# Attention steps 9 to 14 of a fused attention and MLP kernel: three batches of two in place of five visits, and four transpositions in other places

## The chip, the core and the metric

The kernel runs on one core of a Trainium2 chip. The metric is the device time of one execution in microseconds (us). The engines, with the short names of the profile: PE (TensorE, matrix products; PEld is its weight loads), DVE (VectorE), ACT (ScalarE), POOL (GpSimd) and SP (SyncE, which here only issues DMAs). PE writes to PSUM, of which the kernel uses eight banks; DVE and ACT take the results out of it to SBUF.

## What is computed

Linear attention with a decay per head, and an MLP on its output. For 4 batches, 8 heads, 768 positions and head size 64, in blocks of 64 positions:

```python
intra = np.einsum('bhic,bhjc->bhij', qb, kb) * Dmask[None]
intra = np.einsum('bhij,bhjd->bhid', intra, vb)
inter = np.einsum('bhid,bhde->bhie', qb * lam_pow[None], kv_state)
out[:, :, sl] = intra + inter
kv_state = lam_block * kv_state + np.einsum('bhsd,bhse->bhde', kb * rev_pow, vb)
...
h = x @ w_in                      # x: (3072, 512), w_in: (512, 2048)
g = 0.5 * h * (1.0 + np.tanh(c * (h + 0.044715 * h * h * h)))
return g @ w_out                  # w_out: (2048, 512)
```

`x` is the attention output, one row for each batch and position, one column for each head and channel.

## The kernel before, in words

**Steps.** Attention goes in 24 steps (0 to 23). Step s stands for a superblock of 256 positions (s // 2; three to a batch) and one half of the heads (s % 2). A step needs, in this order:

- `load_step(s)`: DMAs of q, k and v on SP's queue, into four buffers each.
- `cast_q(s)` on DVE (line 281, q times a decay, to fp16), `cast_k(s)` on ACT (line 293), `scale_v(s)` on POOL (line 265, v times the inverse decay). `prep_qk(s)` is both casts.
- `stage_t(s)`: eight transpositions on PE (line 309) of q and k into one PSUM bank, then two copies to the tile qkT: q's half on ACT (line 316), k's half on DVE (line 317).
- `scores(s)`: 16 small matmuls (64x64 weights, line 341) into two banks; `causal(s)`: two products with the mask on DVE (line 351), into PT.
- the outputs of a step s: products of v and PT (line 391, or 451 in a burst) and of the state u and q (404 or 413, 479 or 489). Steps in the set NARROW do the second with eight 64x64 matmuls (four for the first superblock of a batch), behind a wait of PE; the others with up to four 128x128 ones. The outputs of s are made one visit later than the scores of s.
- K products of step n (line 376, or 466), which `update(n, c)` adds to the running state on DVE (lines 538, 541), from which POOL makes u (lines 549, 556). `update(n, 0)` is done at the end of a visit, `U(n)` is `update(n, 1)`.
- `x_out`: ACT copies the outputs to xT (lines 518, 520), from which the MLP reads.

**Visits.** `R(n, s)` does the scores, the mask and the K products of step n, and the outputs of step s, in four banks. `burst(ns, ss)` does the same for two steps n and one or two steps s: four banks of scores, two of outputs (O), two of K products, then the masks of both, `x_out` and `update(n, 0)`.

**The MLP as filler.** The MLP is cut into pieces of about 0.87 us on PE, which stand in a list, `filler`; `fill(n)` emits the next n. `queue_group(g)` appends the pieces of a group once its last step is through (group 2 is steps 6 and 7, group 3 is steps 8 to 11, group 4 is steps 12 to 15). A group of one superblock has eight pieces of the first MLP product (line 604), each followed by a GELU on ACT (line 608), and seven pieces of the second (line 683). The second product is done in seven products in place of eight, from sums: `sum_g` (DVE, line 653) makes sums of GELU results and is tied to certain pieces (`behind`): for group 2 to the sixth to eleventh. The pieces of the second product, by their number m, are 1, 2, 5, 6, 3, 7, 4; the bank X0 of 1 serves 6, 7 and 4 too, and is held until 4 is done. DVE adds to the outputs at lines 725 and 731. `sum_win` (DVE, line 150) makes sums of the input weights, needed by later groups, in whose pieces (lines 787 to 817) the first product too is done from sums (line 766 makes those of x), with GELUs at line 805 and additions on DVE at 809.

**Order.** Every instruction is pinned: on each engine, the program's order is the order in the queue. The order of everything is written out by hand in the body of the function (lines 984 to 1203): stage_t, fill, casts, visits, updates, one after another. An engine that waits holds what stands behind it.

Of the kernel before, what the change touches and what calls it, by code (L numbers as in the profile page):

```python
# [15 lines left out]
def kernel(  # L16
# [259 lines left out]
    def cast_q(s):  # L276
        q32 = ld32[s][0]
        tqk = a16p.tile([P, 2, 2, HH, D], FP16, tag="qk16", name=f"qk16_{s}")
        tq, tk = tqk[:, 0], tqk[:, 1]
        q_eng = nc.gpsimd if s == 3 else nc.vector  # L280
        pin(q_eng.tensor_tensor(wide(tq), q32[:], decay(dq, s), ALU.mult))  # L281
        if s == 0:
            inverse(halves[0])
            odd(halves[1])
            inverse(halves[1])
        a16[s] = (tq, tk)

    def cast_k(s):
        tk, k32 = a16[s][1], ld32[s][1]
        if s == 4:  # L290
            pin(nc.vector.tensor_copy(out=wide(tk), in_=k32[:]))
        else:
            pin(nc.scalar.activation(out=wide(tk), in_=k32[:], func=AF.Copy))  # L293
# [5 lines left out]
    def stage_t(s):  # L299
        tq, tk = a16[s][:2]  # L300
        if s < 4:
            Tps = [ps_M.tile([P, 2, 2, P], FP16, tag="M", name=f"Tps{i}") for i in range(2)]
        else:
            Tps = ps_M.tile([P, 2, 2, 2, P], FP16, tag="M", name="Tps")
        for i, t in enumerate((tq, tk)):
            to = Tps[i] if s < 4 else Tps[:, i]
            for hp in range(2):
                for j in range(2):
                    pin(nc.tensor.transpose(to[:, j, hp, :], t[:, j, 2 * hp : 2 * hp + 2, :],  # L309
                                            ident[:]))  # L310
        o = qkp.tile([P, 2, 2, 2, P], FP16, tag="qkT", name=f"qkT_{s}")
        if s < 4:
            pin(nc.scalar.activation(out=o[:, 0], in_=Tps[0][:], func=AF.Copy))
            pin(nc.vector.tensor_copy(out=o[:, 1], in_=Tps[1][:]))
        elif s > 7:
            pin(nc.scalar.activation(out=o[:, 0], in_=Tps[:, 0], func=AF.Copy))  # L316
            pin(nc.vector.tensor_copy(out=o[:, 1], in_=Tps[:, 1]))  # L317
        elif s in (5, 6):
            pin(nc.scalar.activation(out=o[:], in_=Tps[:], func=AF.Copy))
        else:  # L320
            pin(nc.vector.tensor_copy(out=o[:], in_=Tps[:]))
        qkT[s] = o
# [105 lines left out]
    def burst(ns, ss, *mix, ahead=None):  # L428


        narrow = bool(NARROW & set(ss))
        for i, n in enumerate(ns):
            scores(n)
            if ahead and i == 0:
                ahead()
        O = [ps_M.tile([P, 2, 2, P], FP32, tag="M", name=f"O{c}") for c in range(2)]
        seen = set()

        def start(kind, c, hl):
            new = (kind, c, hl) not in seen  # L440
            seen.add((kind, c, hl))
            return new

        qTs = [qkT.pop(s) for s in ss]
        for i, s in enumerate(ss):
            PT, tv = PTs.pop(s), a16.pop(s)[2]
            for hp in range(2):
                for jk in range(2):
                    for c, hl in TILES:
                        to = hl ^ narrow * c  # L450
                        mm = nc.tensor.matmul(  # L451
                            O[c][half64(to), i, hp, :], tv[half64(c), jk, 2 * hp + hl, :],
                            PT[half64(c), hl, hp, jk, :], start=start("O", c, to), stop=False,
                            skip_group_check=True)
                        pin(mm)
        if ns:
            K = [ps_M.tile([P, 2, P], FP32, tag="M", name=f"K{c}") for c in range(2)]
        for i, n in enumerate(ns):
            _, tk, tv = a16[n]
            last = (n // 2) % NSB == NSB - 1  # L460
            for jk in range(2):
                for hp in range(2):
                    for c, hl in TILES:
                        if c == 1 and last:
                            continue
                        pin(nc.tensor.matmul(
                            K[c][half64(hl), i, hp * D : hp * D + D],
                            tk[half64(c), jk, 2 * hp + hl, :], tv[half64(c), jk, 2 * hp + hl, :],
                            start=start("K", c, hl), stop=(jk == 1), skip_group_check=True))
            Kps[n] = [t[:, i] for t in K]  # L470
        if narrow:
            behind(mm)
        for i, s in enumerate(ss) if narrow else ():
            u = [us.pop(key, None) for key in ((s - 2, 1), (s, 0))]
            for hp in range(2):
                for c, hl in TILES:
                    if u[c] is None:
                        continue
                    pin(nc.tensor.matmul(
                        O[c][half64(hl ^ c), i, hp, :], u[c][half64(hl), hp, :],  # L480
                        qTs[i][half64(hl), 0, :, hp, half64(c)], start=False, stop=True,
                        skip_group_check=True))
        for i, s in enumerate(ss) if not narrow else ():
            for c in range(2):
                if c == 0 and (s // 2) % NSB == 0:
                    continue
                u = us.pop((s, 0) if c else (s - 2, 1))
                for hp in range(2):
                    pin(nc.tensor.matmul(O[c][:, i, hp, :], u[:, hp].rearrange("p l d -> p (l d)"),
                                         qTs[i][:, 0, :, hp, half64(c)], start=False, stop=True,  # L490
                                         skip_group_check=True))
        for n in ns:
            causal(n)
        for batch in ((ss,) if narrow or not ns else [(s,) for s in ss]):
            i = ss.index(batch[0])
            x_out(batch, [t[:, i : i + len(batch)].rearrange("p i h t -> p (i h t)") for t in O],
                  swapped=narrow)
        sbg = ss[-1] // 2
        g, i = group_of[sbg]
        if ss[-1] % 2 == 1 and i == len(groups[g]) - 1:  # L500
            queue_group(g, *mix)
        for n in ns:
            update(n, 0)

# [449 lines left out]
    def fill(n):  # L954
        for _ in range(min(n, len(filler))):
            filler.pop(0)()
# [23 lines left out]
    def U(n):  # L980
        update(n, 1)
# [94 lines left out]
    scale_v(9)  # L1076
    fill(2)

    FILL = {8: (2, 0, 0, 0), 9: (1, 2, 1, 2), 10: (0, 1, 1, 3), 11: (0, 1, 1, 3), 12: (0, 2, 1, 3)}
    stage_t(8)  # L1080
    for n, (a, b, c, d) in FILL.items():
        fill(a + (n == 10))
        if n == 8:
            cast_q(n + 2)
            fill(1)
            cast_k(n + 2)
        else:
            prep_qk(n + 2)
        if n < 11:
            load_step(n + 4, "qkv" if n < 10 else "qk")  # L1090
        if n == 11:
            scale_v(13)
            load_step(14, "v")
            load_step(16, "qk")
        elif n == 9:
            scale_v(11)
        elif n == 10:
            scale_v(12)
            load_step(15, "qk")
        elif n == 12:  # L1100
            scale_v(14)
        fill(b + (n == 8) - (n == 10))
        R(n, n - 1, keep=n == 8)
        fill(c)
        if n == 8:
            update(n, 0)
            scale_v(n + 2)
            fill(2)
        U(n)
        if n == 12:  # L1110
            prep_qk(15)
            load_step(15, "v")
            load_step(16, "v")
            scale_v(15)
        stage_t(n + 1)
        fill(d)
        if n > 8:
            sum_win((n - 7) // 2, (n - 1) % 2, nc.vector)

    cast_qk(16)  # L1120
    load_step(17, "qk")
    load_step(17, "v")
    store_pair(1)
    for send in kept_stores[0]:
        send()
    scale_v(16)
    fill(1)
    stage_t(14)
    fill(2)
    burst((13, 14), (12,))  # L1130
    fill(1)
    U(13)
    U(14)
    load_ahead(18)
    fill(1)
    stage_t(15)
    fill(2)
    stage_t(16)
    fill(2)
    burst((15, 16), (13, 14), ahead=lambda: (prep_qk(17), scale_v(17)))  # L1140
    for send in kept_stores[1]:
        send()
# [29 lines left out]

    burst((18, 19), (16, 17))
    prep_v(21)
    fill(2)
    U(18)
    U(19)
    fill(2)
    stage_t(20)
    fill(2)  # L1180
    stage_t(21)
    prep_qk(22)
    fill(2)
    burst((20, 21), (18, 19), 11, 4)
    fill(3)
    U(20)
    U(21)
    fill(20)
    prep_qk(23)
    fill(23)  # L1190
    prep_v(22)
    prep_v(23)
    fill(3)
    stage_t(22)
    fill(4)
    stage_t(23)
    fill(6)
    burst((22, 23), (20, 21))
# [33 lines left out]
```

## Time and profile before

| what | value |
|---|---|
| median of 3 runs | 206.25 us (206.2 to 206.27) |
| the profiled execution | 205.97 us |
| its span, first to last instruction | 204.2 us |
| ACT, busy share of the span | 65% |
| POOL, busy share of the span | 32% |
| HBM, mean over the span | 164 GB/s |

The page of the profile lists busy times, the chain of work that ended last (followed back from the last instruction), and groups of instructions by line. The timeline lists instructions in order of time: start in us from the span's start, time taken by the (merged) entry, engine, line, tiles, shapes and count, and in brackets the idle time ahead of it with what ended it. Matmuls are pipelined, so an entry of PE is longer than the distance to the next start; durations of PE work are therefore taken from start to start, and mostly those of DVE too. The windows view gives, for a stretch, its length and then the busy time of PE, PEld, DVE, ACT and POOL with the number of instructions in brackets, the granted PE clock, and the DMA share and rate.

The attention visits in PE's timeline begin at 58.75 (R(8,7)), 64.48 (R(9,8)), 69.38 (R(10,9)), 75.15 (R(11,10)), 81.80 (R(12,11)), 89.77 (burst (13,14)/(12)), 97.19 (burst (15,16)/(13,14)), 107.16 (R(17,15)), 121.19 (burst (18,19)/(16,17)), 130.62 (burst (20,21)/(18,19)) and 161.12 (burst (22,23)/(20,21)). The transpositions of steps 9 to 16 begin at 61.32, 66.22, 71.12, 76.89, 83.61, 87.51, 92.75 and 94.92; those of 20 to 23 at 126.18, 128.35, 155.15 and 157.34.

### The profile page before, as it was taken

To read this page: it belongs to the slowest core of one execution; us is meant where nothing else is said; L and a number is where in the kernel's file an instruction comes from. 1 tells how busy PE (TensorE), PEld (TensorE's weight loads), DVE (VectorE), ACT (ScalarE), POOL (GpSimd) and SP (SyncE) were. 2 spreads that over 40 slices of the span, in tenths; PEclk is the share of its full clock that TensorE was granted. 3 is DMA by queue.
4 is the path that set the end of the run, shared out by engine and by line. 5 is a ranking of instruction groups with operands and counts; after the bars stand their busy time and mean duration, and the time that the engine had idled before them with its cause. 6 is when DMAs were issued, how large, how long until landed. Compare 5 with 4: busy or idle time off the path is not lost.

```text
span 204.2 us, 6246 instructions
## 1 busy us (share of the span) xinstructions
PE 197.8 (97%) x2597; PEld 146.2 (72%) x2597; DVE 151.4 (74%) x307; ACT 133.7 (65%) x264; POOL 66.3 (32%) x85
## 2 busy tenths in 40 slices
PE   8979999999999999999999999999999999999993
PEld 2556544467888888655588865668889788888882
DVE  5897525789799979969989545999566898467720
ACT  2673867297866896787856389763868665679221
POOL 6684132457407423715224505037001130002000
PEclk9999999999999999999999999999999999999999
DMA  6999999999999477598504480000011200020205
GB/s 180 290 333 389 382 389 370 292 290 290 295 305 249 137 206 216 169 321 226 152 7 121 149 249 6 0 3 0 0 42 64 102 9 0 3 103 2 106 3 203
DMA packets 45916, 33.95 MB, mean 166 GB/s; under 512 B 1728, under 2 KB 38848, under 8 KB 45888
## 3 DMA queue, kind: packets, MB, share of 16 engines
q1 hardware_dynamic: 45344, 33.30, 54.8%
q8 instruction: 20, 0.33, 0.7%
q10 hardware_dynamic: 544, 0.26, 0.4%
q14 instruction: 8, 0.07, 0.1%
HBM read 27.26 MB, written 6.29 MB: 164 GB/s over the span
## 4 chain that ended last, share of the span: by engine, by line
PE 85%; SPq 4%; DMA 4%; ACT 3%; DVE 2%; issue 1%
PE Hps L604 20%; PE MX L683 17%; PE MY L683 9%; PE HX L787 7%; PE O2ps L619 7%; PE MW L683 4%; PE Tps L309 4%; DMA wi<-in_moe_w_in_dram 4%; SPq L69 4%; PE HY L787 4%; PE S L341 3%; PE Hps L886 3%; PE HW L787 2%; DVE gs L653 1%; PE O L451 1%; PE OK L391 1%
## 5 line engine op out<-in xcount | busy, mean ns | idle before, releaser
L604 PE MATMUL Hps<-xT,w_in 128*128 128x512 f16 (+1 forms) x288 | 52.0, 332 | 0.0
L604 PEld LDWEIGHTS <-w_in 128*128 128x128 f16 x288 | 27.3, 98 | 17.6
L608 ACT ACTIVATE gT<-Hps 128x512 f16<-128x512 f32 x56 | 32.7, 598 | 8.9 <-PE Hps L604 8.5
L683 PEld LDWEIGHTS <-gs 128*128 128x128 f16 x320 | 31.1, 98 | 3.7
L351 DVE TENSOR_TENSOR PT<-S,mask 128x512 f16<-128x512 f32 x48 | 30.4, 683 | 3.4 <-PE S L341 3.1
L265 POOL TENSOR_TENSOR v<-v,dv 128x512 f16<-128x512 f32 x24 | 28.2, 1179 | 7.8 <-DMA v<-in_v_dram 4.7
L683 PEld LDWEIGHTS <-gT 128*128 128x128 f16 x240 | 23.1, 98 | 3.5 <-ACT gT L608 0.2
L556 POOL TENSOR_TENSOR u<-t,lumask 128x256 f16<-128x256 f32 x21 | 14.9, 723 | 26.7 <-DVE t L541 15.6
L683 PE MATMUL MX<-w_sum,gs 128*128 128x256 f16 x160 | 21.4, 273 | 0.0
L549 POOL TENSOR_TENSOR u<-t,lamu 128x128 f16<-128x128 f32 x19 | 9.0, 477 | 33.4 <-DVE t L541 27.0
L293 ACT ACTIVATE qk<-k 128x512 f16<-128x512 f32 x23 | 14.4, 626 | 7.7 <-DMA k<-in_k_dram 7.4
L281 DVE TENSOR_TENSOR qk<-q,dq 128x512 f16<-128x512 f32 x23 | 18.4, 798 | 0.7 <-DMA q<-in_q_dram 0.7
L740 POOL TENSOR_TENSOR o<-u,q 128x512 f32<-128x512 f32 (+1 forms) x5 | 5.6, 1119 | 40.0 <-issue 35.1
L653 DVE TENSOR_TENSOR gs<-gT 128x1024 f16<-128x1024 f16 (+1 forms) x24 | 17.1, 721 | 0.5 <-ACT gT L608 0.5
L317 DVE COPY qkT<-Tps 128x512 f16<-128x512 f16 x16 | 6.8, 423 | 12.3 <-ACT qkT L316 12.3
L309 PEld LDWEIGHTS <-qk 128*128 128x128 f16 x192 | 12.8, 99 | 4.2 <-DVE qk L281 0.7
L309 PE MATMUL Tps<-ident,qk 128*128 128x128 f16 x192 | 15.2, 222 | 0.5 <-POOL qk L281 0.5
L619 PE MATMUL O2ps<-w_out,gT 128*128 128x512 f16 x64 | 14.6, 379 | 0.0
L787 PEld LDWEIGHTS <-ws 128*128 128x128 f16 x128 | 12.4, 98 | 1.7 <-DVE xs L766 0.3
L520 ACT ACTIVATE xT<-OK 128x256 f16<-128x256 f32 x22 | 8.7, 454 | 5.1 <-PE OK L413 2.7
L705 ACT ACTIVATE u<-MX 128x256 f32<-128x256 f32 x18 | 6.9, 384 | 7.1 <-PE MX L683 7.1
L619 PEld LDWEIGHTS <-gT 128*128 128x128 f16 x64 | 6.1, 98 | 6.6
(107 smaller groups left out, 350.6 us busy)
## 6 DMA issues: line engine op xcount, KB each, us to landing
q<-in_q_dram SPq DMA_DIRECT2D x24, 256.0 KB, 5.0
k<-in_k_dram SPq DMA_DIRECT2D x24, 256.0 KB, 5.1
v<-in_v_dram SPq DMA_DIRECT2D x23, 256.0 KB, 5.3
out_dram<-o SPq DMA_DIRECT2D x23, 256.0 KB, 2.7
wo<-in_moe_w_out_dram SPq DMA_DIRECT2D x4, 1024.0 KB, 9.5
wi<-in_moe_w_in_dram SPq DMA_DIRECT2D x4, 512.0 KB, 7.8
wi<-in_moe_w_in_dram SPq DMA_DIRECT2D x2, 1024.0 KB, 12.5
v<-in_v_dram ACTq DMA_DIRECT2D x1, 256.0 KB, 4.2
```

The lines of the kernel that those rows point to most:

```text
L265: pin(nc.gpsimd.tensor_tensor(wide(tv[:]), ld32[s][2][:], decay(dv, s), ALU.mult))
L281: pin(q_eng.tensor_tensor(wide(tq), q32[:], decay(dq, s), ALU.mult))
L293: pin(nc.scalar.activation(out=wide(tk), in_=k32[:], func=AF.Copy))
L309: pin(nc.tensor.transpose(to[:, j, hp, :], t[:, j, 2 * hp : 2 * hp + 2, :], ident[:]))
L351: pin(nc.vector.tensor_tensor(t[:, hl].rearrange("p b c d -> p b (c d)"), Sps[:].rearrange("p b c d -> p b (c d)"), mask[:].unsqueeze(1).t ...
L556: pin(nc.gpsimd.tensor_tensor(u[:], state[half][:].unsqueeze(2).to_broadcast([P, 2, 2, D]), lumask[:, 2 * half : 2 * half + 2, :].unsqueez ...
L604: pin(nc.tensor.matmul(by_block(Hps[:, i, :]), w_in16[:, c, f * P : (f + 1) * P], x(c), start=(c == 0), stop=(c == NC - 1)))
L608: pin(nc.scalar.activation(out=dst, in_=Hps[:], func=AF.Gelu_apprx_tanh))
L619: pin(nc.tensor.matmul(O2[tau][0][:], gT[:, f % HF, f // HF, tau * P : (tau + 1) * P], w_out16[:, f, :], start=(n == 0), stop=(n == NF - 1)))
L653: pin(nc.vector.tensor_tensor(g_rows(m, i), g_rows(a, i), g_rows(b, i), op))
L683: pin(nc.tensor.matmul(dst, lhsT, rhs, start=(opens and i == 0), stop=(closes and i == HF - 1), skip_group_check=True))
L787: pin(nc.tensor.matmul(dst[:, i, :], w_in_block(a, slice(c, c + 1), slice(f * P, f * P + P))[:, 0], x_block(b, slice(c, c + 1))[:, 0], sta ...
```

## The change

The loop over steps 8 to 12 with its table FILL is written out. R(8,7) stays. R(9,8), R(10,9), R(11,10), R(12,11) and burst (13,14)/(12) become burst (9,10)/(8), burst (11,12)/(9,10) and burst (13,14)/(11,12). Casts, loads, value scalings, weight sums and pieces of filler take new places around them; their number is the same. `burst` queues a group for each of its steps s, not for the last one alone (step 11, the end of group 3, is now the first of two). The transpositions of 20, 21 and 22 stand earlier; those of 23 stand behind the same pieces, but both halves of their result are copied by ACT in one instruction, where before ACT copied one and DVE the other.

```diff
@@ stage_t
-        elif s > 7:
+        elif 7 < s < 23:
             pin(nc.scalar.activation(out=o[:, 0], in_=Tps[:, 0], func=AF.Copy))
             pin(nc.vector.tensor_copy(out=o[:, 1], in_=Tps[:, 1]))
-        elif s in (5, 6):
+        elif s in (5, 6, 23):
             pin(nc.scalar.activation(out=o[:], in_=Tps[:], func=AF.Copy))
@@ burst
-        sbg = ss[-1] // 2
-        g, i = group_of[sbg]
-        if ss[-1] % 2 == 1 and i == len(groups[g]) - 1:
-            queue_group(g, *mix)
+        for s in ss:
+            g, i = group_of[s // 2]
+            if s % 2 == 1 and i == len(groups[g]) - 1:
+                queue_group(g, *mix)
@@ the order, steps 8 to 16
-    FILL = {8: (2, 0, 0, 0), 9: (1, 2, 1, 2), 10: (0, 1, 1, 3), 11: (0, 1, 1, 3), 12: (0, 2, 1, 3)}
     stage_t(8)
-    for n, (a, b, c, d) in FILL.items():
-        fill(a + (n == 10))
...
-        R(n, n - 1, keep=n == 8)
...
-        if n > 8:
-            sum_win((n - 7) // 2, (n - 1) % 2, nc.vector)
+    fill(2)
+    cast_q(10)
+    fill(1)
+    cast_k(10)
+    load_step(12)
+    fill(1)
+    R(8, 7, keep=True)
+    update(8, 0)
+    scale_v(10)
+    fill(2)
+    U(8)
+    stage_t(9)
+    fill(1)
+    prep_qk(11)
+    load_step(13)
+    scale_v(11)
+    fill(2)
+    stage_t(10)
+    fill(2)
+    burst((9, 10), (8,))
+    fill(1)
+    U(9)
+    U(10)
+    prep_qk(12)
+    load_step(14, "qk")
+    scale_v(12)
+    load_step(15, "qk")
+    fill(2)
+    sum_win(1, 0, nc.vector)
+    stage_t(11)
+    fill(2)
+    sum_win(1, 1, nc.vector)
+    stage_t(12)
+    fill(2)
+    burst((11, 12), (9, 10))
+    fill(1)
+    U(11)
+    U(12)
+    prep_qk(13)
+    scale_v(13)
+    load_step(14, "v")
+    load_step(16, "qk")
+    fill(2)
+    sum_win(2, 0, nc.vector)
+    stage_t(13)
+    prep_qk(14)
+    scale_v(14)
+    fill(2)
+    sum_win(2, 1, nc.vector)
+    stage_t(14)
+    fill(1)
+    burst((13, 14), (11, 12))
+    fill(1)
+    U(13)
+    U(14)
+    prep_qk(15)
+    load_step(15, "v")
+    load_step(16, "v")
+    scale_v(15)
+    fill(4)
     cast_qk(16)
...
     scale_v(16)
-    fill(1)
-    stage_t(14)
-    fill(2)
-    burst((13, 14), (12,))
-    fill(1)
-    U(13)
-    U(14)
+    fill(3)
     load_ahead(18)
-    fill(1)
     stage_t(15)
     fill(2)
     stage_t(16)
-    fill(2)
+    fill(3)
     burst((15, 16), (13, 14), ahead=lambda: (prep_qk(17), scale_v(17)))
@@ the order, steps 20 to 23
     burst((18, 19), (16, 17))
     prep_v(21)
+    stage_t(20)
     fill(2)
     U(18)
     U(19)
-    fill(2)
-    stage_t(20)
-    fill(2)
     stage_t(21)
+    fill(4)
     prep_qk(22)
     fill(2)
     burst((20, 21), (18, 19), 11, 4)
     fill(3)
     U(20)
     U(21)
+    stage_t(22)
     fill(20)
     prep_qk(23)
     fill(23)
     prep_v(22)
     prep_v(23)
-    fill(3)
-    stage_t(22)
-    fill(4)
+    fill(7)
     stage_t(23)
     fill(6)
     burst((22, 23), (20, 21))
```

More of the change, by code (lines that the diff above doesn't have):

```diff
@@ L1077 @@
     fill(2)
-    FILL = {8: (2, 0, 0, 0), 9: (1, 2, 1, 2), 10: (0, 1, 1, 3), 11: (0, 1, 1, 3), 12: (0, 2, 1, 3)}
     stage_t(8)
-    for n, (a, b, c, d) in FILL.items():
-        fill(a + (n == 10))
-        if n == 8:
-            cast_q(n + 2)
-            fill(1)
[L1086 to L1102, printed above, removed]
-        R(n, n - 1, keep=n == 8)
[L1104 to L1107, printed above, removed]
-            fill(2)
[L1109 to L1116, printed above, removed]
-        if n > 8:
-            sum_win((n - 7) // 2, (n - 1) % 2, nc.vector)
+    fill(2)
[58 more added lines that the diff above has]
+    fill(4)
     cast_qk(16)
-    load_step(17, "qk")
-    load_step(17, "v")
+    load_step(17)
     store_pair(1)
@@ L1126 @@
     scale_v(16)
-    fill(1)
-    stage_t(14)
-    fill(2)
-    burst((13, 14), (12,))
-    fill(1)
-    U(13)
-    U(14)
+    fill(3)
     load_ahead(18)
-    fill(1)
     stage_t(15)
@@ L1177 @@
     U(19)
-    fill(2)
-    stage_t(20)
-    fill(2)
     stage_t(21)
+    fill(4)
     prep_qk(22)
```

## The prediction

> **What bounds the kernel now.** I read the page first, then the chain of waits, then TensorE's timeline around the attention visits, then VectorE's and GpSimd's.
>
> ```profile
> PE 197.8 (97%) x2597; PEld 146.2 (72%) x2597; DVE 151.4 (74%) x307; ACT 133.7 (65%) x264; POOL 66.3 (32%) x85
> PE 85%; SPq 4%; DMA 4%; ACT 3%; DVE 2%; issue 1%
> ```
>
> TensorE (PE) is busy 97% of the span and is 85% of the chain that ended last: from 18 us on each PE instruction follows the one before it. So the time is PE's work plus PE's stalls, and nothing later takes a stall back. The granted clock is 1.00 in every window I read. VectorE (DVE) looks free at 74%, but that is a mean. The view of busy time by windows says for the stretch that is changed:
>
> ```profile
> 75.10:81.80 6.70, 6.70 (x106) 5.78 (x105) 6.70 (x15) 4.43 (x10) 1.67 (x2) 1.00 0.63 186
> ```
>
> DVE (third busy column) is busy 6.70 of 6.70 us. It keeps up there only because what PE needs next was put well ahead in DVE's queue.
>
> PE's timeline of one visit, R(10,9), and of a burst of two steps over two steps (columns: start, time, line):
>
> ```profile
> 69.38 0.25 PE L376 MATMUL OK<-v,qk 64*64 64x64 f16 x4
> ...
> 70.24 1.05 PE L604 MATMUL Hps<-xT,w_in 128*128 128x256 f16 x8
> ...
> 121.19 0.64 PE L341 MATMUL S<-qkT 64*64 64x128 f16 x32
> ...
> 122.71 3.63 PE L604 MATMUL Hps<-xT,w_in 128*128 128x512 f16 x16
> ```
>
> The visit is from its first start to that of the next MLP matmul: 70.24-69.38 = 0.86 us; the burst, 1.52 us.
>
> DVE, before and behind the burst at 89.77, and a collision:
>
> ```profile
> 75.57 0.69 DVE L281 TENSOR_TENSOR qk<-q,dq 128x512 f16<-128x512 f32 x1
> ...
> 61.73 1.26 DVE L653 TENSOR_TENSOR gs<-gT 128x512 f16<-128x512 f16 x1
> ...
> 90.23 2.48 DVE L351 TENSOR_TENSOR PT<-S,mask 128x512 f16<-128x512 f32 x4 [0.84 <-PE S L341]
> 92.64 0.28 DVE L538 COPY t<-K 128x128 f32<-128x128 f32 x1
> ```
>
> The first is step 13's query cast; it runs at 75.57 for transpositions at 83.61, 8 us ahead. Four masks of a burst hold DVE 92.64-90.23 = 2.41 us, longer than the burst holds PE. The line at 61.73 took 1.26 us where its like takes 0.42 (56.30): GpSimd (POOL) was in its value scaling from 61.48 to 62.71.
>
> **Part 1: what merging the visits saves on PE.** Matmul counts stay. Before, from the starts: R(9,8) 0.86, R(10,9) 0.86, R(11,10) 0.86, R(12,11) 0.93, burst (13,14)/(12) 1.25; sum 4.76. After: burst (9,10)/(8) is the 1.25 one with two wide state matmuls (0.11) replaced by eight narrow and their wait (0.14: R(9,8) is 0.86, R(8,7) without its two wide ones 0.82-0.11 = 0.71): 1.28. Burst (11,12)/(9,10) is like that at 121.19: 1.52. Burst (13,14)/(11,12) has 16 more products than the 1.25 one, at 1.52/112 = 13.6 ns each, 0.22, and six wide matmuls for two, 0.22: 1.69. Sum 4.49: 0.27 saved. Ahead of each visit stands an entry cost: 24 matmuls before R(10,9) last 69.38-66.67 = 2.71 where three pieces at 0.873 are 2.62, so 0.09; two fewer visits save 0.18. Together **-0.45 us**. The filler pieces until burst (15,16) are equally many (31 after R(8,7)), and the queue is never empty: one piece is left when group 3 is queued, before and after.
>
> **Part 2: what the new order asks of DVE.** All instructions keep program order on their engine, so I walk the DVE queue. Until R(8,7) nothing moves. From its end (59.58) I lay out PE with pieces of 0.873 and transpositions of 0.445: burst (9,10) starts at 66.7, transpositions of 12 at 72.8, burst (11,12) at 75.05, ending at 76.6; then three pieces, and step 13's transpositions want to start at 79.2.
>
> DVE meanwhile, start to start from rows: mask 0.60, state update 0.19 a half, SBUF sum 0.34, cast 0.60, out-sum 0.33, weight sum (L150) 0.60, qkT copy 0.34. The eighth mm1 piece of group 2 ends at 75.0; its GELU ends about 75.8 (0.2 wait and 0.6); the sum tied to that piece (line 653) stands on DVE ahead of the masks, as it does before (76.17). So masks start at 76.2, not 75.5, and end at 78.6. Then update 11 (0.39), update 12 (0.19), a sum (0.34), U(12) (0.39), and only then the cast of q for 13 (0.60): done at 80.55, with its write about 80.65. PE waits: 80.65-79.2 = **+1.45 us**. (A part of it, 0.4, appears already behind the burst: burst (11,12) takes all eight PSUM banks, and the first bank comes free with the first mask, 76.9, not 76.6.) If the sum weren't late it would be 0.8; if POOL's state products (0.40 to 0.73) block the cast as 63.63's 0.83 shows, 1.75.
>
> Step 14: behind cast 13 DVE has an out-sum, two sums, a weight sum, a qkT copy and cast 14: 0.33+0.34+0.34+0.60+0.34+0.60 = 2.55 us; PE has 0.445+1.75 = 2.2. So +0.35 without collisions. But POOL runs the value scalings of 13 and 14 back to back from about 80.8 to 83.2 (1.04 to 1.57 each), over these very sums. The rows give +0.84 (61.73) and +0.54 (85.57: 1.22 for 0.68) for a collision; one collision costs about 0.7, two 1.5. I take one, the middle: **+1.05 us**; ends 0.35 and 1.85.
>
> The Trainium skill, "SBUF — State Buffer", section "Who interferes with whom", says that a DVE instruction with two SBUF inputs and a GpSimd one that reads SBUF exclude each other for the whole instruction, whichever is first. By that rule alone both scalings would block in full, and this term would be at its upper end, 1.85. The rows show less in some places (L150 at 85.57), so I stay at one.
>
> Burst (13,14): its second scores wait for the qkT copy of 14 (ACT 0.6, then DVE 0.42 behind the transposition, and only one piece, 0.87, between): +0.15. Product bank X0 of group 2 is still open across it (pieces 7 and 4 stand on either side), so seven banks are there for eight tiles, and the last waits for the first mask: +0.1. **+0.25.** No burst in this trace runs with a product bank open, so the ends are 0 and 0.6 (one mask). xT of step 11 isn't late: PE has 0.87 and two half-matmul sets ahead of its use, ACT's two copies take 0.77.
>
> Behind it, 12 pieces follow as before; cast 15 and 16 have 7 us for 5 us of DVE. Burst (15,16) now has two sums after its last transposition: I take +0.1 (0 to 0.8, with one collision). ACT's work in 75-84 (eight copies and casts, about 4.5 us) isn't late for any of these. On SP, loads of 18 stand behind stores that wait for group 2's last piece, now 5 us later, at 89; step 18 is used at 105, loads land in 5 us: nothing. Loads 14 to 17 are freed by casts of steps four earlier, and are 5 us early or more.
>
> The Trainium skill, "Trainium Kernel Development and Optimization", section "Best Practices", speaks against the change: packing small matmuls speeds TensorE but not the evacuation of PSUM. It gives no price; the row does: 2.41 us of masks to 1.52 us of burst.
>
> **Part 3: steps 20 to 23.** Burst (20,21) took 132.47-130.62 = 1.85; by the terms above 96 x 13.6 ns + 4 wide (0.22) = 1.53. It waited about 0.3 for step 21's qkT copy on DVE (130.69), which stood behind four sums of 0.7. With both transpositions two to four pieces earlier the copy comes before the sums: **-0.28**. What is late next, the first GELU behind the ACT copy of 20, 0.5 later, has free banks. Step 22's pair of copies (0.6 ACT, 0.34 DVE) moves to 135, where DVE's x sums aren't read for 4 us: nothing. At 157.79 to 161.12 six pieces took 3.33 us where they need 2.63+0.09: HX at 160.59 waited for DVE's q (159.85, L809), which stood behind step 23's qkT copy (158.92, itself waiting 0.72 for ACT). That copy goes to ACT, 22's is gone; q then follows its matmul (159.1), ends at 160.0: **-0.55** (0 to -0.6). ACT pays 1.02 for 0.64 there, and has lost 22's 0.6.
>
> **Sum.** -0.45 -0.28 -0.55 = -1.28; +1.45 +1.05 +0.25 +0.1 = +2.85; net +1.57. Against the profiled execution's 205.97 us (span 204.2) that is 207.5; the median 206.25 lies 0.28 above that execution, so 207.8.
>
> **Rivals.** *DVE comes in time (faster, 20%)*: the stalls at 13 and 14 are under 1.07 together, the point from which sign turns (the other two terms kept at a small 0.2). For it: DVE sits idle about 1.9 us ahead of the first burst's masks, and its mean load in 59.58 to 82.86 is 21.04 of 23.28 us. Against: the order is fixed, and without any lateness the list alone gives 0.8+0.35. Price: gains alone 1.28, less 0.2 to 0.7 of rest: 205.4. *Double collisions (slower still, 20%)*: both scalings hit DVE and the bank in burst (13,14) waits a whole mask: 1.75+1.85+0.6+0.5 = 4.7, net +3.4: 209.6. *Nothing but the saved switches, cancelled (8%)*: stalls about 1.3: 206.25. My own case has 52%, 206.7 to 208.8.
>
> The measurement tells about 0.2% (0.41 us) from no change. Faster by more 0.18 (the first rival less its slowest tenth), within 0.10 (that tenth and the last rival), slower 0.72 (my case and the second rival). The range: low end with the stalls of a list without lateness and half the faster case, 205.7; high end well into the collisions, 209.4.
>
> **What would show it.** Right: PE idle ahead of line 309 between 79 and 85, released by DVE's L281, 2 us or more in sum; masks in fours right before it; three attention visits of 1.3 to 1.7 in place of five; no wait for q L809 near 160; burst (20,21) at 1.55. Wrong: PE without a gap ahead of those transpositions, or DVE's cast of 13 finished before 79.2; or the tail's stalls still there.

## The result and the profile after

The changed kernel takes 208.61 us (median of 4 runs, 208.51 to 208.63) against 206.26 beside it: 1.0108 times, 95% interval 1.0091 to 1.0126, so 2.35 us slower. Its profiled execution took 208.62 us, span 206.8. From the page: busy shares, and the chain that ended last by engine; then the windows view of the stretch of batches two and three.

```profile
PE 197.8 (96%) x2597; PEld 146.2 (71%) x2597; DVE 149.6 (72%) x306; ACT 133.4 (64%) x261; POOL 68.4 (33%) x85
PE 86%; SPq 4%; DMA 4%; DVE 4%; issue 1%; ACT 0%; DVEq 0%
```

```profile
75.50:86.66 11.16, 8.15 (x171) 6.84 (x170) 10.75 (x24) 6.01 (x11) 5.02 (x5) 1.00 0.47 143
```

PE's sum is the same, 197.8 us; DVE has doubled its share of the chain. In the window PE works 8.15 of 11.16 us: 3.0 us of idle, where the kernel before had next to none. DVE is busy 10.75. The waits view of PE for 57 to 110 names the releasers (total, times, longest), and PE's and DVE's timelines show the places:

```profile
PE Tps L309 <- DVE qk L281: 2.8, 2, 1.8
PE MX L683 <- DVE PT L351: 0.2, 1, 0.2
```

```profile
64.67 0.61 PE L309 MATMUL Tps<-ident,qk 128*128 128x128 f16 x8
65.31 1.03 PE L683 MATMUL MX<-w_sum,gT 128*128 128x256 f16 x8
...
77.31 1.03 PE L683 MATMUL MX<-w_out,gT 128*128 128x256 f16 x8 [0.24 <-DVE PT L351]
...
79.06 1.04 PE L683 MATMUL MY<-w_sum,gs 128*128 128x256 f16 x8
81.04 0.62 PE L309 MATMUL Tps<-ident,qk 128*128 128x128 f16 x8 [0.95 <-DVE qk L281]
81.50 1.04 PE L683 MATMUL MX<-w_sum,gs 128*128 128x256 f16 x8
82.37 1.04 PE L683 MATMUL MY<-w_out,gs 128*128 128x256 f16 x8
85.23 0.62 PE L309 MATMUL Tps<-ident,qk 128*128 128x128 f16 x8 [1.82 <-DVE qk L281]
```

```profile
75.82 0.84 DVE L653 TENSOR_TENSOR gs<-gT 128x512 f16<-128x512 f16 x2
76.58 2.48 DVE L351 TENSOR_TENSOR PT<-S,mask 128x512 f16<-128x512 f32 x4
...
80.27 0.72 DVE L281 TENSOR_TENSOR qk<-q,dq 128x512 f16<-128x512 f32 x1
...
82.20 1.53 DVE L150 TENSOR_TENSOR ws<-ws,w_in 128x1024 f16<-128x1024 f16 x1
83.65 0.41 DVE L317 COPY qkT<-Tps 128x512 f16<-128x512 f16 x1
83.98 1.19 DVE L281 TENSOR_TENSOR qk<-q,dq 128x512 f16<-128x512 f32 x1
```

The second of the two sums at 75.82 is the one tied to the eighth GELU. The cast of q for step 13 runs at 80.27, right behind the masks and updates, and PE's transpositions follow it at 81.04; the cast for step 14 ends at 85.17, and the transpositions follow at 85.23. The 0.64 us between the first two lines of PE's fence are step 10's transpositions (0.445) and a wait of 0.19 before product 4. While the weight sum (82.20, 1.53 us; alone 0.68) and that cast (1.19; alone 0.68) run, POOL scales v of 13 and 14:

```profile
81.96 2.67 POOL L265 TENSOR_TENSOR v<-v,dv 128x512 f16<-128x512 f32 x2
```

In the last part the waits are gone: burst (20,21), and the pieces behind step 23's transpositions up to the burst at 163.77.

```profile
134.14 0.64 PE L341 MATMUL S<-qkT 64*64 64x128 f16 x32
...
135.67 0.59 PE L604 MATMUL Hps<-xT,w_in 128*128 128x512 f16 x2
...
160.99 0.60 PE L787 MATMUL HY<-xT,ws 128*128 128x256 f16 x4
...
163.24 0.60 PE L787 MATMUL HX<-xs,w_in 128*128 128x256 f16 x4
163.77 0.64 PE L341 MATMUL S<-qkT 64*64 64x128 f16 x32
```

From R(8,7) on, PE's starts close the account. R(8,7) itself starts 0.29 later than before (59.04, 58.75), in code that the change doesn't touch. The profiled execution of the kernel before lies 0.28 us under its median, and in every other kept trace R(8,7) starts later than in it (58.82 to 59.14); so the table leaves that out.

| part, on PE | before | after | difference | predicted |
|---|---|---|---|---|
| visits of steps 9 to 14, without their waits | 4.75 | 4.37 | -0.38 | -0.27 |
| two entry costs | 0.19 | 0 | -0.19 | -0.18 |
| product 4 behind step 10's transpositions | 0 | 0.19 | +0.19 | 0 |
| step 13: bank behind burst (11,12) 0.30, transpositions 1.11 | 0 | 1.41 | +1.41 | +1.45 |
| ahead of step 14's transpositions | 0 | 1.98 | +1.98 | +1.05 |
| inside burst (13,14) | 0 | 0.31 | +0.31 | +0.25 |
| burst (15,16) | 1.60 | 1.51 | -0.09 | +0.10 |
| steps 20 to 23 (1.85 to 1.53; 3.33 to 2.78) | 5.18 | 4.32 | -0.86 | -0.83 |
| sum | | | +2.37 | +1.57 |

The 4.37 is the sum of 1.24, 1.51 and 1.62: what burst (9,10) took in the changed kernel, and the shortest that the other two took in any run below.

### The profile page after: what moved, and what is told of

Same layout as the page of the kernel before. It is cut to its first block, busy times and chain, and to the rows that moved or that the text cites. A ratio compares the mean times of both kernels' runs of the same rounds, so it can differ in the third digit from the quotient of the medians.

```text
span 206.8 us, 6238 instructions
## 1 busy us (share of the span) xinstructions
PE 197.8 (96%) x2597; PEld 146.2 (71%) x2597; DVE 149.6 (72%) x306; ACT 133.4 (64%) x261; POOL 68.4 (33%) x85
## 4 chain that ended last, share of the span: by engine, by line
PE 86%; SPq 4%; DMA 4%; DVE 4%; issue 1%; ACT 0%; DVEq 0%
PE Hps L604 24%; PE MX L683 16%; PE MY L683 8%; PE HX L787 7%; PE O2ps L619 7%; PE Tps L309 4%; DMA wi<-in_moe_w_in_dram 4%; PE MW L683 4%; SPq L69 4%; PE HY L787 3%; PE S L341 3%; PE Hps L886 3%; PE HW L787 2%; PE O L451 2%; PE K L466 1%; DVE PT L351 1%
## 5 line engine op out<-in xcount | busy, mean ns | idle before, releaser
L265 POOL TENSOR_TENSOR v<-v,dv 128x512 f16<-128x512 f32 x24 | 29.0, 1215 | 7.6 <-DMA v<-in_v_dram 7.2
L683 PEld LDWEIGHTS <-gT 128*128 128x128 f16 x240 | 23.2, 98 | 3.5 <-issue 0.2
L556 POOL TENSOR_TENSOR u<-t,lumask 128x256 f16<-128x256 f32 x21 | 15.9, 775 | 26.6 <-DVE t L541 16.3
L281 DVE TENSOR_TENSOR qk<-q,dq 128x512 f16<-128x512 f32 x23 | 17.6, 769 | 0.7 <-DMA q<-in_q_dram 0.7
L317 DVE COPY qkT<-Tps 128x512 f16<-128x512 f16 x15 | 6.3, 421 | 14.0 <-ACT qkT L316 14.0
L520 ACT ACTIVATE xT<-O 128x256 f16<-128x256 f32 (+1 forms) x15 | 7.7, 574 | 7.2 <-PE O L479 3.6
L316 ACT ACTIVATE qkT<-Tps 128x512 f16<-128x512 f16 x15 | 9.0, 598 | 5.0 <-PE Tps L309 4.8
```

Of the source, the lines that this page charges most:

```text
L265: pin(nc.gpsimd.tensor_tensor(wide(tv[:]), ld32[s][2][:], decay(dv, s), ALU.mult))
L556: pin(nc.gpsimd.tensor_tensor(u[:], state[half][:].unsqueeze(2).to_broadcast([P, 2, 2, D]), lumask[:, 2 * half : 2 * half + 2, :].unsqueez ...
L683: pin(nc.tensor.matmul(dst, lhsT, rhs, start=(opens and i == 0), stop=(closes and i == HF - 1), skip_group_check=True))
```

## The experiments

The theory: PE waits because DVE, in its fixed order, reaches two casts late; the length of its queue, a sum that waits for a GELU ahead of the masks, and POOL's scalings decide how late. The rivals: the place of the casts alone; the banks; no gain at all in the visits or the tail. Line numbers shift by a few in kernels that add lines.

**e1_tail and e2_batches: the two halves alone.** The first is the kernel before with the diff's edits to `stage_t` and to steps 20 to 23, shown above whole; the second is the changed kernel without them:

```diff
-        elif 7 < s < 23:
+        elif s > 7:
...
-        elif s in (5, 6, 23):
+        elif s in (5, 6):
...
-    stage_t(20)
     fill(2)
     U(18)
     U(19)
+    fill(2)
+    stage_t(20)
...
```

> The kernel before, with the change's edits to steps 20 to 23 alone. Theory of the prediction: the two late copies on VectorE go, burst (20,21) falls from 1.85 us to 1.53 and the six pieces behind step 23's transpositions from 3.33 to 2.8; together 0.86, so 205.4 us. Rival (these waits only hide another one right behind them): within 0.2% of 206.25.

> The changed kernel, with steps 20 to 23 as before: the batches alone. Theory: all of the loss and 0.45 us of gain are in the batches, so 208.61 + 0.86 = 209.5 us. Rival (the tail's gain depends on the batches, or isn't there): 208.6.

Measured: 205.38 us, ratio 0.9962 (0.9949 to 0.9976); 209.49, 1.0159 (1.0146 to 1.0173). The halves add: -0.8 and +3.3 make +2.5 by these medians, 2.35 is measured together. The tail's gain is real, and all of the loss is in the batches.

**e11_t23: steps 22 and 23 alone**, in the kernel before:

```diff
-        elif s > 7:
+        elif 7 < s < 23:
...
-        elif s in (5, 6):
+        elif s in (5, 6, 23):
...
     U(21)
+    stage_t(22)
     fill(20)
...
-    fill(3)
-    stage_t(22)
-    fill(4)
+    fill(7)
     stage_t(23)
```

> The kernel before, with the edits to steps 22 and 23 alone. Theory: of the tail's 0.81 these two give 0.55 (VectorE reaches q at line 809 earlier, nothing waits for it), steps 20 and 21 the rest: 205.65. Rival (the two parts only work together, as the second wait hides behind the first): 206.2.

Measured: 205.71, 0.9977 (0.9967 to 0.9987). In its trace the six pieces take 2.78 us and burst (20,21) still 1.86: the two waits of the tail are independent.

**e3_scale: POOL's scalings out of DVE's way**

```diff
-    burst((11, 12), (9, 10))
+    burst((11, 12), (9, 10), mid=lambda mm: (scale_v(13, mm), scale_v(14, mm)))
...
     prep_qk(13)
-    scale_v(13)
...
     prep_qk(14)
-    scale_v(14)
```

`mid` is called ahead of the burst's updates; each scaling waits for the burst's last product of v and PT. The load of v for step 14 moves ahead of the burst with them.

> The changed kernel; the value scalings of steps 13 and 14 run on GpSimd behind the products of burst (11,12), under VectorE's four masks, instead of behind the state products, over VectorE's sums and step 14's cast. Nothing of VectorE's own queue is changed. Theory (the scalings exclude VectorE's instructions with two SBUF inputs; a mask has one, its other comes from PSUM): the sum at 82.20 takes 0.68 for 1.53 and cast 14 0.69 for 1.19, the wait ahead of step 14's transpositions falls from 1.94 us to 0.5, so 207.2 us; the wait at step 13 stays at 1.4. Rival (VectorE is late by its own work, the scaling makes no difference): 208.6. Second rival (the masks are slowed too): 208.6 or more, with masks over 0.68.

Measured: 207.38, 1.0058 (1.0044 to 1.0072), 1.2 us less than the change. DVE and POOL:

```profile
76.58 2.48 DVE L355 TENSOR_TENSOR PT<-S,mask 128x512 f16<-128x512 f32 x4
...
79.56 0.85 DVE L659 TENSOR_TENSOR gs<-gs,gT 128x512 f16<-128x512 f16 x1
...
82.35 0.68 DVE L150 TENSOR_TENSOR ws<-ws,w_in 128x1024 f16<-128x1024 f16 x1
...
83.29 0.68 DVE L285 TENSOR_TENSOR qk<-q,dq 128x512 f16<-128x512 f32 x1
```

```profile
76.74 2.04 POOL L265 TENSOR_TENSOR v<-v,dv 128x512 f16<-128x512 f32 x2 [2.84 <-issue]
79.52 1.36 POOL L562 TENSOR_TENSOR u<-t,lumask 128x256 f16<-128x256 f32 x2 [0.73 <-DVE t L547]
```

The masks take 2.48 us for four with the scalings beside them, as without; the weight sum and the cast are back at 0.68. The wait ahead of step 14's transpositions is 0.34 in this trace (84.02-81.94, the starts of its transpositions and of the first piece ahead of them, less 1.74 for two pieces). Step 13's wait grew by 0.44, which I hadn't expected: POOL's state product now starts at 79.52, 0.04 ahead of DVE's sum, which takes 0.85 for 0.42. In the changed kernel the sum started first (79.55; POOL 79.60) and took 0.42. So POOL's scalings did hold DVE up, which of two colliding instructions is held depends on which starts first, and both rivals fall.

**e4_sums: a shorter DVE queue**

```diff
-    sum_win(1, 0, nc.vector)
     stage_t(11)
...
-    sum_win(2, 1, nc.vector)
     stage_t(14)
...
     scale_v(16)
+    for m in (1, 2):
+        for j in range(2):
+            sum_win(m, j, nc.vector)
```

> The changed kernel; the four weight sums (line 150) of steps 9 to 14 stand behind step 16's value scaling, where VectorE idles from 93 to 98. Theory (VectorE's queue is too long between burst (9,10) and step 14's transpositions; whatever leaves it shortens the wait, until the sum tied to the eighth piece holds the masks): wait at step 13 from 1.4 to 1.0, at step 14 from 1.94 to 0.4, so 206.7 us. Rival (the places of the two casts behind the masks alone are at fault, not the queue's length): waits nearly as they are, 208 or more.

Measured: 207.13, 1.0044 (1.0030 to 1.0058). The wait at step 14 fell to 0.53; that at step 13 not at all (transpositions at 81.04 again). DVE's timeline says why:

```profile
76.22 0.43 DVE L653 TENSOR_TENSOR gs<-gT 128x512 f16<-128x512 f16 x1 [0.61 <-ACT gT L608]
76.57 2.48 DVE L351 TENSOR_TENSOR PT<-S,mask 128x512 f16<-128x512 f32 x4
```

With two sums fewer ahead of the burst DVE stands idle for 0.61 us, until the eighth GELU; the masks start where they did (76.57 for 76.58). So the queue's length makes most of the wait at 14. At 13 the tied sum is enough to hold the masks, however short the queue. In the changed kernel both limits met: that GELU ends at 76.20 there, and DVE reaches the sum without idle time, held up by its own queue until about then. My expectation of 0.4 less there was wrong: I had counted on the sums ahead of the masks, behind which that wait was hidden.

**e5_casts and e6_sums_casts: the casts one visit earlier, alone and with the former edit**

```diff
     stage_t(12)
+    prep_qk(13)
     fill(2)
     burst((11, 12), (9, 10))
...
     U(12)
-    prep_qk(13)
+    prep_qk(14)
...
     stage_t(13)
-    prep_qk(14)
```

> The changed kernel; the casts of steps 13 and 14 stand one visit earlier: 13's behind step 12's transpositions, ahead of the masks of burst (11,12), 14's where 13's stood. Rival theory (the place of these two casts alone makes the loss): both waits ahead of transpositions go, 3.3 us less, 205.3. Theory (VectorE's queue is also too long there, so what is put ahead holds up what stands behind): the wait at step 13 goes, but masks start 0.6 later, the bank behind burst (11,12) comes 0.6 later, the sums of the products and the qkT copy of 14 are late in the casts' place; 207.4.

> The changed kernel with both of the former edits: the four weight sums behind step 16's value scaling, and the two casts one visit earlier. Theory: the masks of burst (11,12) start no later than in the changed kernel, since they wait for the sum tied to the GELU at 76.2 anyway; no wait ahead of either transposition; what is left is 0.24 for the bank behind burst (11,12), up to 0.5 ahead of product 3 for the sums that the value scalings slow, 0.25 in burst (13,14): 206.0. If the two edits only added what each brings alone, it would be lower or higher by what they share.

Measured: 207.60, 1.0069 (1.0055 to 1.0083), and 205.61, 0.9974 (0.9964 to 0.9984). With the casts alone PE waits elsewhere (waits of e5_casts):

```profile
PE S L341 <- DVE qkT L317: 1.4, 2, 1.0
PE MX L683 <- DVE PT L351: 0.8, 1, 0.8
```

The transpositions no longer wait, but the bank behind burst (11,12) and step 14's qkT copy do: 2.2 us, most of the 3.1 that the casts saved. So the casts' place alone isn't the cause. The casts bring 1.0 alone, the sums 1.5, both together 3.0: each takes away what the other leaves, and no wait ahead of either transposition is left. The batches then no longer lose anything that can be told: 205.61 stands beside the tail's 205.38, with intervals that overlap.

**e7_all and e8_all_bank**

e6's moves with e3's scalings, the tied sum (`late[0]`) between the masks of 11 and 12, and cast 14 behind the product sums; then e8 on top of e7:

```diff
-    burst((11, 12), (9, 10))
+    burst((11, 12), (9, 10), mid=lambda mm: (scale_v(13, mm), scale_v(14, mm)), split=late[0])
...
     fill(2)
+    prep_qk(14)
     stage_t(13)
```

```diff
     stage_t(14)
-    fill(1)
+    fill(2)
     burst((13, 14), (11, 12))
-    fill(1)
```

> The changed kernel with weight sums later, step 13's cast ahead of burst (11,12) and 14's behind the product sums, the value scalings of 13 and 14 under the masks, and the sum that waits for the eighth GELU put between the two steps' masks. Theory: all waits between 75 and 87 go but for 0.2 in burst (13,14); what stays is the gain of the tail (0.81 by the run of the tail alone) and of the merged visits (0.45): 205.0, below the tail alone (205.4). Rival (merging the visits saves nothing on TensorE, the entry costs are elsewhere): 205.4 or more.

> The run before this one, with both last pieces of group 2 ahead of burst (13,14) and none behind it. Theory of the prediction on banks: product bank X0 is closed then, burst (13,14) has its eight banks and its qkT copy in time, 0.2 less inside the burst. But the piece that covered ACT's copies of step 11's outputs is gone: group 3's first product waits for xT by 0.3 to 0.6. Net 0.1 to 0.4 more than the run before. Rival (the bank matters more than the cover): less than the run before.

Measured: 206.13, 0.9998 (0.9989 to 1.0007), a miss by 1.1 us; 206.95, 1.0043 (1.0030 to 1.0055). DVE in e7_all:

```profile
79.72 0.85 DVE L662 TENSOR_TENSOR gs<-gs,gT 128x512 f16<-128x512 f16 x1
...
82.03 0.68 DVE L285 TENSOR_TENSOR qk<-q,dq 128x512 f16<-128x512 f32 x1
```

POOL's state product was first again (79.67), so the sums that products 6 and 3 read came late, and the cast of 14, put behind them, later still: from step 13's transpositions to step 14's PE lost 0.98, of it 0.33 in the wait for the cast. In e8_all_bank burst (13,14) takes 1.62 for 1.93, so the open bank X0 and the late copy together cost 0.31 there. By the starts of its parts it is 0.12 in the scores, where the copy of step 14 was late (0.47 for 0.59), and 0.19 in the K products, where the last bank waited for the first mask (0.36 for 0.55). But product 4, now right behind 7, waits 0.5 for ACT's copy out of X0, and group 3's first product 0.2 for xT (PE's waits).

**e9_split, e10_swap, e12_order: from 205.61 on**

Each adds to the one before, e9 to e6:

```diff
-    burst((11, 12), (9, 10))
+    burst((11, 12), (9, 10), split=late[0])
```

```diff
     stage_t(10)
+    filler[:2] = filler[1::-1]
     fill(2)
```

```diff
     U(12)
-    prep_qk(14)
...
-    fill(2)
+    fill(1)
+    prep_qk(14)
+    fill(1)
     stage_t(13)
```

> The run with weight sums later and casts earlier (205.61), and the sum tied to the eighth GELU put between the masks of step 11 and those of step 12. Theory (this sum, which waits for its GELU until 76.2, is what holds the masks and through them the bank behind burst (11,12)): masks start up to 0.4 earlier, the wait of 0.24 for the bank goes, the next places have 0.3 to spare, 205.35. Rival (what is saved there is lost at product 3, whose sums come later): 205.6 or more.

> The run before this one, and group 1's last piece changes places with group 2's first, so that a piece stands between product 7 and product 4, which share bank X0. Theory: the 0.19 that TensorE waits behind step 10's transpositions (for ACT's copy out of X0) goes: 0.19 less than the run before, about 205.15. Rival (burst (9,10) then waits for that bank itself): no less than the run before.

> The run before this one, with the cast of step 14 one place later on VectorE, behind the addition of product 2 and the sum that product 3 reads. Theory: in that run the six pieces behind step 13's transpositions lose 0.3 ahead of product 3, because its sum stands behind the cast; the cast has 0.3 to spare ahead of step 14's transpositions. So 0.3 less: 205.0. Rival (the cast is late now, and TensorE waits at the transpositions instead): 205.3.

Measured: 205.56, 0.9965 (0.9951 to 0.9978); 205.27, 0.9954 (0.9941 to 0.9966); 205.41, 0.9954 (0.9938 to 0.9970). In e9 the wait for the bank is gone (burst (11,12) 1.51 for 1.82), the masks start at 76.19 for 76.59, and 0.2 of it is lost again in the middle of product 3, which waits for its sum, as its rival said: its median is 0.05 lower, less than can be told. In e10 product 4 no longer waits, and burst (9,10) isn't longer (1.21). In e12 product 3 no longer waits, but the cast and the sum that product 7 reads met POOL's products and the first scaling (from 80.96):

```profile
80.66 0.88 DVE L281 TENSOR_TENSOR qk<-q,dq 128x512 f16<-128x512 f32 x1
81.47 1.26 DVE L656 TENSOR_TENSOR gs<-gT 128x512 f16<-128x512 f16 x1
```

so of the 0.3 gained at product 3, 0.23 went in step 14's transpositions, which wait for the cast as the rival said, and another 0.3 was lost at product 7. The expectation of 0.3 less failed. The best version of the batches, e10, is about 0.95 us faster than the kernel before; the tail alone is 0.8 faster, and their intervals overlap. It isn't shown that the batches bring anything beyond the tail. Their 0.57 on PE is there in e10's trace; of it, 0.31 is lost in burst (13,14) and 0.31 in product 3's wait for its sum (2.06 for 1.75, from step 13's first piece to step 14's transpositions).

## Why the prediction was right, and where it was off

- **What bounds the kernel, right.** PE's sum of busy time didn't move by 0.1 us; the difference is PE's waits and switches. (The pieces between R(8,7) and burst (15,16) are 33, not 31, before and after; that they are equally many, on which the sum rests, holds.)
- **Part 1, right.** -0.57 for -0.45: the three bursts take 1.24, 1.51 and 1.62 where I had 1.28, 1.52 and 1.69.
- **Part 2, step 13: right in mechanism and size**, 1.41 for 1.45. The cause named holds too: masks held to 76.58 by the sum that waits for the eighth GELU (e4 shows DVE idle there), then the list of updates and the cast. That the wait would be 0.8 without this sum isn't shown: DVE's own queue reached it no earlier, and no run moves that sum alone in this order.
- **Part 2, step 14: right in mechanism, the term mis-sized.** The list without collisions was 0.35, and e3 measures 0.34. I counted one collision of 0.7; there were two, 0.85 on the weight sum and 0.5 on the cast, and about 0.28 more where POOL's state products met the two product sums: 1.98. The choice of one came from a row (85.57) in which less of the scaling was left when DVE came: 0.68 us by POOL's own row, of which DVE lost 0.54; in the changed kernel 0.98 was left (the scaling's row is 81.96, 1.22), of which it lost 0.85. The section of the Trainium skill that I cited ("SBUF — State Buffer", "Who interferes with whom") would have put the term at its upper end, 1.85, and was nearer: what comes second waits until the first is through. The trace before also showed this very pair, and the prediction uses only its first half:

```profile
85.57 1.22 DVE L150 TENSOR_TENSOR ws<-ws,w_in 128x1024 f16<-128x1024 f16 x1
86.72 1.52 DVE L281 TENSOR_TENSOR qk<-q,dq 128x512 f16<-128x512 f32 x1
```

```profile
85.21 2.49 POOL L265 TENSOR_TENSOR v<-v,dv 128x512 f16<-128x512 f32 x2
```

Two scalings back to back held up a weight sum by 0.54 and the cast behind it by 0.84, 1.38 in all; in the changed kernel it is 0.85 and 0.5, 1.35. With both collisions from these rows the term would have been 0.35+1.38 = 1.73.

- **Burst (13,14), right**: 0.31 for 0.25; the copy of 14 cost 0.12 for 0.15, the open bank 0.19 for 0.1 (e8).
- **Missed:** product 4 waits 0.19 behind step 10's transpositions, since R(9,8) no longer stands between it and product 7, which share a bank (e10, with a piece between them, has no such wait). Burst (15,16) lost nothing; it gained 0.09, for which no run shows a cause.
- **Part 3, right**: -0.86 for -0.83, each part by itself (e1, e11).
- The stalls came to 3.9 us of waits and the gains to 1.5: net 2.4, between the 1.57 of my case and the 3.4 of the second rival. 208.61 lies inside my case's 206.7 to 208.8, close to its slow end. Of the distance of 0.80 step 14's term makes 0.93; that the missed 0.19 and burst (15,16)'s 0.19 cancel is luck.

## What to carry to other kernels

When TensorE is full and one evacuating engine nearly so, the worth of a merge is read from that engine's queue: list what stands on it between the merged block and the next thing that TensorE needs, and put that ahead of the block, together with moving out what nobody needs yet; of the 3.0 us that the two brought here, the one alone gave 1.0 and the other 1.5. Look for an instruction that waits (here a sum for a GELU) right ahead of a long batch: put between the masks, it let them start 0.4 us earlier, though most of that was lost again further on. Place the other engine's conflicting work beside instructions that read PSUM, and check the new neighbours: a collision that is moved can meet another instruction, as POOL's state product did here.

## What the runs showed of the hardware

- A start 0.04 us earlier decides who pays: the same sum took 0.42 us (POOL's state product 0.05 behind, which then took 0.83) and 0.85 (POOL's product 0.04 ahead, taking 0.61).
- Masks with one operand in PSUM weren't slowed by POOL's value scalings: 2.48 us for four, with two scalings beside them (e3) and with POOL idle (the burst at 90.23 before). The scalings weren't slowed either, 2.04 us for two.
